# Attention score columns in a new order, one exp and three masks per step, and the rearrangement of Wo moved ahead in the DMA queue

## The chip, the cores and the metric

The kernel runs on one core of one Trainium2 chip. A time is the device time of one execution, in microseconds (us). The core has a matmul engine (PE; its weight loads are told apart as PEld), a vector engine (DVE), an engine for activation functions (ACT), a general one (POOL), and a queue engine (SP) that here does nothing but issue DMAs. The engines run on their own and wait for each other through semaphores.

## The reference

A block that adds three things: its input, sliding-window attention on the layer-normed input, and a gated linear unit (GLU) on the same normed input. There are 2048 positions, 640 features, 32 heads of 20, a window of 256 positions, and 1536 hidden features.

```python
xn = _layernorm(x)
# attention: H = 32, Dh = 20, W = 256
q, k, v = (xn @ wqkv) split into heads
scores = einsum("bhqd,bhkd->bhqk", q, k) * Dh ** -0.5
mask = (q_pos - k_pos >= 0) & (q_pos - k_pos < W)
p = softmax(where(mask, scores, -1e9))
attn = einsum("bhqk,bhkd->bhqd", p, v) reshaped to (B, S, D) @ wo
# GLU
h = sigmoid(xn @ w_gate) * (xn @ w_up)
return x + attn + h @ w_down
```

All data are bfloat16. B_x is not used.

## The kernel before, in words

**Chunks and fillers.** The 2048 positions are cut into four chunks of 512 (`c` = 0 to 3). Chunk 0 is normed, transposed and projected first (L601 to L633). Then one loop (L665 to L690) walks through the attention steps of all chunks and puts "filler" matmuls between them: the gate and up products (`g_gu`, L392), the q, k and v projections of the next chunk (`g_qk`, L360, and `g_v`, L375), and the down product with Wo's product added into the same PSUM tile (`g_out`, L448). The fillers stand in one list (L643 to L661), each with a cost in ns; a `credit` shared out evenly over the steps says how much of the list is taken after each step. A filler that only issues a DMA costs 0 and is taken when its turn in the list comes. So the order on every engine is fixed when the program is built, and each engine works its list off in order.

**Attention steps.** Four heads form a group `g`, and there are eight groups. A step takes scores between blocks of 128 keys and the queries they may see. Queries are counted in units of 64; a key block is used in halves of 64 keys (`hf` 0 and 1), which land in the lower and upper 64 partitions. One entry of `scores` is (group, half, key block relative to the chunk, first query unit, number of units, PSUM column unit), and becomes four matmuls, one per head, of 20 x 64 weights (L463). A step fills 8 column units for each of the four heads: the tile `ps`, four PSUM banks, of which there is one buffer. A chunk after the first has per pair of groups five steps: two "old" wide steps for each group, which also touch the previous chunk's keys, and one "full" step for both groups, which needs no mask. Chunk 0 has two wide steps per group. That makes 16 + 3 x 20 = 76 steps, 48 of them old wide ones.

**Exp and masks.** ACT takes `ps` through exp into the bfloat16 tile `pT` (L469), ten units wide; there are four buffers. In a wide step the first exp takes five units and the second three, which it writes one unit further on. POOL's `affine_select` (L473) then puts zeros where a key is later than the query or older than the window. `late` copies a masked unit to a unit of its own, since one unit holds scores of a first half of keys for one block and of a second half for another; `oldest` and `diag` mask in place. An old wide step has six masks (four of 64 columns per head, two of 128), a wide step of chunk 0 four.

**PV.** Two steps after a group's last one, `pv` (L489) multiplies V with the group's `pT` pieces: each entry of `pv` is (group, key block, first query unit, units, `pT` column unit) and becomes four matmuls with 128 x 32 weights, one per head, side by side in the array (L494). A column of constants beside V gives the softmax sums. DVE transposes the result, divides, and transposes back into `oc` (L502 to L520).

**DMAs.** All but three are issued by SP, in program order. q and k of a chunk are cast from PSUM into `st` (five buffers; q by DVE, L300, k by ACT, L302), stored to a scratch tensor in DRAM (`sq`, `sk`, L304), and read back with another spread over partitions (`spread`, L311). Wo's rows have to be put in the order in which `oc` holds the heads: `turn_wo` (L218) copies Wo inside DRAM to `wo_i`, four DMAs, and `load_wo` (L223) brings it into SBUF, four DMAs that wait for the first four. `load_wd` (L215) brings the down weights. In the list of fillers `turn_wo` stands after chunk 1's V projection and `load_wo` after the next two gate products, just ahead of `out0`, the first user of Wo.

Of the kernel before, what the change touches and what calls it, by code (L numbers as in the profile page):

```python
# [9 lines left out]
P = 128  # L10
# [7 lines left out]
CW = 512  # L18
NCH = S // CW
SBC = CW // P  # L20
HG = 4
# [6 lines left out]
SCALE = DH ** -0.5  # L28
# [14 lines left out]
U = 64  # L43
# [10 lines left out]

def wide_step(g, r, old):

    q = 2 * r  # L60
    scores = [(g, 0, r, q, 5, 0)]
    if old:
        scores += [(g, 1, r, q + 1, 5, 1), (g, 1, r - 2, q + 1, 1, 0), (g, 0, r + 2, q + 4, 2, 5),
                   (g, 1, r + 2, q + 5, 1, 6), (g, 1, r - 2, q, 1, 7), (g, 0, r - 2, q, 1, 7)]
        return dict(scores=scores, exps=[(0, 5, 0), (5, 3, 6)], late=[(0, 9), (6, 5)], diag=[0, 6],
                    oldest=[4, 8], pv=[(g, r, q, 6, 0), (g, r + 2, q + 4, 2, 6), (g, r - 2, q, 2, 8)],
                    units=8)

    scores += [(g, 1, r, q, 6, 0)]
    if r == 0:  # L70
        scores += [(g, 0, 2, 4, 3, 5), (g, 1, 2, 5, 2, 6)]
        last = [(g, 2, 4, 3, 6)]
    else:
        scores += [(g, 0, 3, 6, 2, 5), (g, 1, 3, 7, 1, 6), (g, 0, 2, 7, 1, 7), (g, 1, 2, 7, 1, 7)]
        last = [(g, 3, 6, 2, 6), (g, 2, 7, 1, 8)]
    return dict(scores=scores, exps=[(0, 5, 0), (5, 3, 6)], late=[(6, 5)], diag=[0, 6], oldest=[4],
                pv=[(g, r, q, 6, 0)] + last, units=8)


def full_step(gs):  # L80

    out = dict(scores=[], exps=[], late=[], diag=[], oldest=[], pv=[], units=8)
    for n, g in enumerate(gs):
        out["exps"].append((4 * n, 4, 4 * n))
        for r, q, col in ((-1, 0, 4 * n), (2, 6, 4 * n + 2)):
            out["scores"] += [(g, hf, r, q, 2, col) for hf in range(2)]
            out["pv"].append((g, r, q, 2, col))
    return out


def steps_of(c):
# [20 lines left out]
def kernel(  # L112
# [11 lines left out]
    nc = tc.nc  # L124
# [41 lines left out]
    wo = const.tile([P, DC, D], BF16, name="wo")  # L166
# [38 lines left out]
    wo_i = tc.dram_tile([HG, NG * DH, D], BF16, name="wo_i")  # L205
# [31 lines left out]
    for n in (7, 6):  # L237
        ps = ps_d.tile([P, CW], FP32, name="pwarm", tag="d")
# [50 lines left out]
    def proj_block(w, c, m):  # L289


        base = 0 if w == "q" else D
        ps = ps_d.tile([P, CW], FP32, name="pqk", tag="d")
        for d in range(DC):
            wt = wqkv[:, d, base:base + D].rearrange("p (k m) -> p m k", m=DC)
            nc.tensor.matmul(ps, lhsT=wt[:, m, :], rhs=xnT[c][:, d, :],  # L296
                             start=(d == 0), stop=(d == DC - 1))
        st = stp.tile([P, CW], BF16, name="st")
        if w == "q":
            nc.vector.tensor_copy(out=st, in_=ps)  # L300
        else:
            nc.scalar.copy(out=st, in_=ps)  # L302
        dst = scratch[w, c % 2].rearrange("(h j) s -> h j s", j=32)
        nc.sync.dma_start(out=dst[:, 4 * m:4 * m + 4, :], in_=st)  # L304
# [142 lines left out]
    def g_out(c):  # L447
        for s in range(SBC):  # L448
            ys = [ps_d.tile([P, CW], FP32, name=f"y{i}", tag="d") for i in range(2)]
            for y, cut in zip(ys, HALVES):  # L450
                yield from down(c, s, y, cut)
            outp(c, s, ys)
            yield 10 * 136


    def scores(c, step):
        pt = pp.tile([P, HG, PTW], BF16, name="pT")
        ps = ps_s.tile([P, HG, CW], FP32, name="ps")
        for g, hf, r, q, n, col in step["scores"]:
            kc, kb = divmod(c * SBC + r, SBC)  # L460
            key = kb * P + hf * U
            for i in range(HG):
                nc.tensor.matmul(  # L463
                    ps[hf * U:(hf + 1) * U, i, col * U:(col + n) * U],
                    lhsT=qk["k", kc][32 * i:32 * i + DH, g, key:key + U],
                    rhs=qk["q", c][32 * i:32 * i + DH, g, q * U:(q + n) * U],
                    start=True, stop=True)
        for col, n, to in step["exps"]:
            nc.scalar.activation(out=pt[:, :, to * U:(to + n) * U], in_=ps[:, :, col * U:(col + n) * U],  # L469
                                 func=EXP, scale=SCALE)  # L470

        def keep(out, in_, pattern, base, sign):
            nc.gpsimd.affine_select(out=out, in_=in_, pattern=[[0, HG], [sign, pattern]], compare_op=GE,  # L473
                                    fill=0.0, base=base, channel_multiplier=-sign)

        def cols(u, n):
            return pt[:, :, u * U:u * U + n]

        for a, b in step["late"]:
            keep(cols(b, U), cols(a, U), U, -1 - U, -1)  # L480
        for u in step["oldest"]:
            keep(cols(u, U), cols(u, U), U, -1, -1)
        for u in step["diag"]:
            keep(cols(u, P), cols(u, P), P, 0, 1)
        return pt

    def pv(c, g, parts):
# [175 lines left out]
    todo = [(c, k, step) for c in range(NCH) for k, step in enumerate(steps_of(c))]  # L663
# [9 lines left out]
    credit = 0  # L673
    fill.shut = {"out0", "out1", "out2"}
    for t, (c, k, step) in enumerate(todo):
        if k == 0 and c > 0:
            fill.until(f"qk{c}")
        if k == 2 and c > 0:
            fill.until(f"v{c}")
        for group in [x for x in ends if ends[x] == t - 2]:  # L680
            fill.flush()
            pv(*group, parts.pop(group))
            if group[1] == NG - 1:
                fill.shut.discard(f"out{group[0]}")
# [4 lines left out]
        credit += fill.left(label) * step["units"] / sum(x[2]["units"] for x in todo[t:last])  # L689
        credit = fill.pull(credit)  # L690
    fill.pull(10 ** 9)
    fill.flush()
# [61 lines left out]
```

## Time and profile before

| what | value |
|---|---|
| median of 5 runs | 317.62 us (317.17 to 319.85) |
| the profiled execution, its own time | 317.62 us |
| its span, first to last instruction | 315.7 us |
| granted clock of PE | 1.00 |
| busy: PE, ACT, POOL, DVE | 308.8, 198.0, 178.9, 154.3 us |
| L463 scores, matmuls | 2048 |
| L494 PV, matmuls | 928 |
| L469 exp, L473 masks, instructions | 152, 352 |

The profile page gives for each engine the busy time, its share of the span and its instructions; then the chain of work that ended last, and the costliest groups of instructions by source line. In a row of groups stand line, engine, operation, what it writes and reads, shapes and count, then the busy time in us, the mean of one in ns, and the idle time before them with what ended it. A row of waits says which instruction waited for which, the total in us, how often, and the longest. A row of the timeline has the start and the duration in us, engine, line, operation, tiles, shape and count; like instructions in succession are merged into one row, and an idle time ahead of it stands in brackets with what ended it. The duration of a matmul in these rows reaches beyond the start of the next one, because matmuls are pipelined; from one row's start to the next row's start is what the first one cost.

### The profile page before, as it was taken

Reading aid. Unit: us, or ns where it says so; the run is one execution under the profiler, and the core shown is the slowest. Engines: PE = TensorE matmul, PEld = TensorE weight load, DVE = VectorE, ACT = ScalarE, POOL = GpSimd, SP = SyncE. Lnnn points to the kernel's source line nnn. Section 1 sums busy time; section 2 is a strip of 40 time slices with the busy share of each in tenths; the row PEclk is TensorE's granted clock in tenths of the full one; section 3 lists DMA queues with packets and bytes.
Section 4 is the critical chain, followed back from the end, with each engine's and each line's share of the span. In section 5 each row is a group of like instructions: output and inputs, shape, how many; then the busy total and the mean of one; then the engine's idle time right before and its main releaser. Section 6 shows DMA issues by size and latency. Waiting matters only on the chain.

```text
span 315.7 us, 10314 instructions
## 1 busy us (share of the span) xinstructions
PE 308.8 (98%) x4410; PEld 175.2 (56%) x4410; DVE 154.3 (49%) x313; ACT 198.0 (63%) x255; POOL 178.9 (57%) x417
## 2 busy tenths in 40 slices
PE   7999999999979999999999999999999999999996
PEld 2654444456556655644466655544456664444674
DVE  3531486654854563347753542444552433563234
ACT  5724887788845458677744457776765658878200
POOL 3000487667758648565975647466365767676300
PEclk9999999999999999999999999999999999999999
DMA  7986958837735255410036025600000010000002
GB/s 254 374 292 190 334 191 131 302 92 208 249 102 65 50 172 153 157 65 2 0 43 88 23 87 142 227 3 2 3 3 23 25 42 3 2 2 2 0 2 83
DMA packets 34572, 33.05 MB, mean 105 GB/s; under 512 B 9920, under 2 KB 33984, under 8 KB 34496
## 3 DMA queue, kind: packets, MB, share of 16 engines
q1 hardware_dynamic: 34096, 32.14, 35.1%
q8 instruction: 34, 0.56, 0.8%
q10 hardware_dynamic: 432, 0.28, 0.3%
q14 instruction: 10, 0.08, 0.1%
HBM read 21.00 MB, written 10.26 MB: 99 GB/s over the span
## 4 chain that ended last, share of the span: by engine, by line
PE 89%; DMA 6%; ACT 2%; SPq 1%; issue 1%; DVE 0%; ACTq 0%
PE pu L403 16%; PE pg L396 16%; PE y L417 14%; PE pqk L296 13%; PE ps L463 8%; PE acc L494 7%; PE y L424 6%; PE pv L322 5%; DMA wo_i<-in_A_wo_dram 2%; PE d L417 2%; DMA sk<-st 1%; DMA wo<-wo_i 1%; DMA xc<-in_A_x_dram 1%; ACT pT L469 1%; SPq L220 1%
## 5 line engine op out<-in xcount | busy, mean ns | idle before, releaser
L473 POOL TENSOR_SCALAR_AFFINE_SELECT pT<-pT 128x256 bf16<-128x256 bf16 (+1 forms) x352 | 164.9, 502 | 115.0 <-ACT pT L469 114.8
L469 ACT ACTIVATE pT<-ps 128x1280 bf16<-128x1280 f32 (+2 forms) x152 | 147.4, 1022 | 64.9 <-PE ps L463 63.7
L407 DVE SCALAR_TENSOR_TENSOR h<-th,pu 128x512 bf16<-128x512 f32 x48 | 32.8, 684 | 56.6 <-PE pu L403 34.9
L396 PE MATMUL pg<-xnT,wg 128*128 128x512 bf16 x240 | 59.8, 380 | 0.0
L403 PE MATMUL pu<-xnT,wu 128*128 128x512 bf16 x240 | 59.8, 380 | 0.0
L417 PE MATMUL y<-wd,h 128*128 128x320 bf16 (+1 forms) x348 | 50.2, 297 | 0.0
L296 PE MATMUL pqk<-xnT,wqkv 128*128 128x512 bf16 x200 | 46.0, 381 | 0.0
L417 PEld LDWEIGHTS <-h 128*128 128x128 bf16 x396 | 36.7, 98 | 14.1 <-issue 0.2
L504 DVE STREAM_TRANSPOSE t<-acc 128x512 f32<-128x512 f32 x32 | 22.8, 712 | 33.5 <-PE acc L494 33.3
L399 ACT ACTIVATE th<-pg 128x512 f32<-128x512 f32 x48 | 28.8, 600 | 14.4 <-PE pg L396 7.7
L403 PEld LDWEIGHTS <-wu 128*128 128x128 bf16 x240 | 22.0, 98 | 25.4 <-issue 0.6
L396 PEld LDWEIGHTS <-wg 128*128 128x128 bf16 x240 | 22.0, 98 | 24.8 <-issue 0.4
L463 PEld LDWEIGHTS <-kT 20*64 20x64 bf16 x2048 | 22.1, 104 | 19.6 <-issue 16.2
L463 PE MATMUL ps<-qT,kT 20*64 20x64 bf16 (+3 forms) x2048 | 32.8, 232 | 0.0
L296 PEld LDWEIGHTS <-wqkv 128*128 128x128 bf16 x200 | 22.5, 119 | 17.9 <-issue 0.6
L428 DVE SCALAR_TENSOR_TENSOR xn<-y,xc 128x320 bf16<-128x320 f32 (+1 forms) x29 | 13.9, 483 | 31.2 <-PE y L424 31.1
L494 PE MATMUL acc<-pT,v 128*32 128x128 bf16 (+2 forms) x928 | 25.7, 250 | 0.0
L494 PEld LDWEIGHTS <-v 128*32 128x32 bf16 x928 | 16.9, 97 | 15.3 <-issue 11.0
L322 PE MATMUL pv<-wqkv,xnT 128*128 128x320 bf16 x160 | 23.8, 300 | 0.0
L424 PE MATMUL y<-wo,oc 128*128 128x320 bf16 (+1 forms) x145 | 21.6, 296 | 1.7 <-DMA wo<-wo_i 1.7
L516 DVE TENSOR_TENSOR on<-t,rec 128x320 bf16<-128x320 f32 (+4 forms) x48 | 20.9, 435 | 1.1
L424 PEld LDWEIGHTS <-oc 128*128 128x128 bf16 x165 | 15.5, 98 | 7.8 <-issue 2.0
(49 smaller groups left out, 148.8 us busy)
## 6 DMA issues: line engine op xcount, KB each, us to landing
qT<-sq SPq DMA_DIRECT2D x3, 1024.0 KB, 5.9
sq<-st SPq DMA_DIRECT2D x20, 128.0 KB, 3.5
sk<-st SPq DMA_DIRECT2D x20, 128.0 KB, 3.8
out_dram<-xn SPq DMA_DIRECT2D x15, 160.0 KB, 1.8
kT<-sk SPq DMA_DIRECT2D x3, 768.0 KB, 5.5
wg<-in_B_w_gate_dram SPq DMA_DIRECT2D x2, 960.0 KB, 7.1
wu<-in_B_w_up_dram SPq DMA_DIRECT2D x2, 960.0 KB, 12.3
xc<-in_A_x_dram SPq DMA_DIRECT2D x3, 640.0 KB
```

What stands on the lines that cost most here:

```text
L296: nc.tensor.matmul(ps, lhsT=wt[:, m, :], rhs=xnT[c][:, d, :], start=(d == 0), stop=(d == DC - 1))
L322: nc.tensor.matmul(ps[:, 0:HALF], lhsT=xnT[c][:, d, s * P:(s + 1) * P], rhs=wqkv[:, d, 2 * D + hf * HALF:2 * D + (hf + 1) * HALF], start=( ...
L396: nc.tensor.matmul(pg, lhsT=part(wg, d, f), rhs=xnT[c][:, d, :], start=(d == 0), stop=(d == DC - 1))
L399: nc.scalar.activation(out=th, in_=pg, func=TANH, scale=0.5)
L403: nc.tensor.matmul(pu, lhsT=part(wu, d, f), rhs=xnT[c][:, d, :], start=(d == 0), stop=(d == DC - 1))
L407: nc.vector.scalar_tensor_tensor(out=h, in0=th, scalar=1.0, in1=pu, op0=ADD, op1=MULT)
L417: nc.tensor.matmul(y[:, 0:cut[1] - cut[0]], lhsT=ht[c, f][:, s * P:(s + 1) * P], rhs=wd[:, f, cut[0]:cut[1]], start=(f == 0), stop=False)
L424: nc.tensor.matmul(y[:, 0:cut[1] - cut[0]], lhsT=oc[c, m][:, s * P:(s + 1) * P], rhs=wo[:, m, cut[0]:cut[1]], start=False, stop=(m == DC - 1))
L463: nc.tensor.matmul(ps[hf * U:(hf + 1) * U, i, col * U:(col + n) * U], lhsT=qk["k", kc][32 * i:32 * i + DH, g, key:key + U], rhs=qk["q", c] ...
L469: nc.scalar.activation(out=pt[:, :, to * U:(to + n) * U], in_=ps[:, :, col * U:(col + n) * U], func=EXP, scale=SCALE)
L473: nc.gpsimd.affine_select(out=out, in_=in_, pattern=[[0, HG], [sign, pattern]], compare_op=GE, fill=0.0, base=base, channel_multiplier=-sign)
L494: nc.tensor.matmul(acc[32 * i:32 * i + 32, q * U:(q + n) * U], lhsT=v[:, h * VW:h * VW + 32], rhs=pt[:, i, col * U:(col + n) * U], start=( ...
```

## The change

In `wide_step` the PSUM columns of an old step are ordered anew. Entries that were two narrow ones are merged, so that there are six score entries, three of them for each half of keys; the masked units now lie in pairs that are five units apart (`SPAN`), so one `affine_select` with a third pattern dimension covers two places. The exp is one instruction over all 8 units and writes `pT` units 0 to 7; units 8 and 9 hold the masked copies. The PV list has more and narrower entries: five for an old step (5, 2, 1, 1 and 1 units) where there were three (6, 2, 2), and one more in each wide step of chunk 0. A full step keeps its scores and PV entries and also gets one exp. In the list of fillers `turn_wo` moves from behind chunk 1's V projection to right behind `load_wd`, and `load_wo` from behind the two gate products to ahead of them. The credit is shared evenly per step, which it was already since every step had 8 units.

```diff
 def wide_step(g, r, old):
     q = 2 * r
-    scores = [(g, 0, r, q, 5, 0)]
     if old:
-        scores += [(g, 1, r, q + 1, 5, 1), (g, 1, r - 2, q + 1, 1, 0), (g, 0, r + 2, q + 4, 2, 5),
-                   (g, 1, r + 2, q + 5, 1, 6), (g, 1, r - 2, q, 1, 7), (g, 0, r - 2, q, 1, 7)]
-        return dict(scores=scores, exps=[(0, 5, 0), (5, 3, 6)], late=[(0, 9), (6, 5)], diag=[0, 6],
-                    oldest=[4, 8], pv=[(g, r, q, 6, 0), (g, r + 2, q + 4, 2, 6), (g, r - 2, q, 2, 8)],
-                    units=8)
+        return dict(scores=[(g, 0, r, q, 5, 1), (g, 1, r, q + 1, 5, 2), (g, 0, r + 2, q + 4, 2, 6),
+                            (g, 1, r - 2, q, 2, 0), (g, 0, r - 2, q, 1, 0), (g, 1, r + 2, q + 5, 1, 7)],
+                    late=(1, 8, 2), diag=1, oldest=(0, 2),
+                    pv=[(g, r, q, 5, 1), (g, r + 2, q + 4, 2, 6), (g, r, q + 5, 1, 9),
+                        (g, r - 2, q, 1, 0), (g, r - 2, q + 1, 1, 8)])
...
-        last = [(g, 3, 6, 2, 6), (g, 2, 7, 1, 8)]
-    return dict(scores=scores, exps=[(0, 5, 0), (5, 3, 6)], late=[(6, 5)], diag=[0, 6], oldest=[4],
-                pv=[(g, r, q, 6, 0)] + last, units=8)
+        last = [(g, 3, 6, 2, 5), (g, 2, 7, 1, 7)]
+    return dict(scores=scores, late=(5, 9, 1), diag=0, oldest=(4, 1),
+                pv=[(g, r, q, 5, 0), (g, r, q + 5, 1, 9)] + last)
...
-        for col, n, to in step["exps"]:
-            nc.scalar.activation(out=pt[:, :, to * U:(to + n) * U], in_=ps[:, :, col * U:(col + n) * U],
-                                 func=EXP, scale=SCALE)
-
-        def keep(out, in_, pattern, base, sign):
-            nc.gpsimd.affine_select(out=out, in_=in_, pattern=[[0, HG], [sign, pattern]], compare_op=GE,
-                                    fill=0.0, base=base, channel_multiplier=-sign)
...
-        for a, b in step["late"]:
-            keep(cols(b, U), cols(a, U), U, -1 - U, -1)
-        for u in step["oldest"]:
-            keep(cols(u, U), cols(u, U), U, -1, -1)
-        for u in step["diag"]:
-            keep(cols(u, P), cols(u, P), P, 0, 1)
+        nc.scalar.activation(out=pt[:, :, 0:CW], in_=ps, func=EXP, scale=SCALE)
+
+        def keep(out, in_, n, width, base, sign):
+            nc.gpsimd.affine_select(out=out, in_=in_, pattern=[[0, HG], [0, n], [sign, width]],
+                                    compare_op=GE, fill=0.0, base=base, channel_multiplier=-sign)
+
+        def spans(u, n, units):
+            a, b = divmod(u, SPAN)
+            two = pt.rearrange("p h (a b) -> p h a b", a=2)
+            return two[:, :, a:a + n, b * U:(b + units) * U]
+
+        if "late" in step:
+            src, to, n = step["late"]
+            keep(pt[:, :, to * U:(to + n) * U].rearrange("p h (n u) -> p h n u", u=U),
+                 spans(src, n, 1), n, U, -1 - U, -1)
+            u, n = step["oldest"]
+            keep(spans(u, n, 1), spans(u, n, 1), n, U, -1, -1)
+            keep(spans(step["diag"], 2, 2), spans(step["diag"], 2, 2), 2, P, 0, 1)
...
     fill.add("wd", later(load_wd), 0)
+    fill.add("wo_i", later(turn_wo), 0)
     fill.add("qk1", g_qk(1), 50 * MM)
     fill.add("v1", g_v(1), 40 * 136)
-    fill.add("wo_i", later(turn_wo), 0)
+    fill.add("wo", later(load_wo), 0)
     fill.add("gu1a", mix(g_gu(1, 0, 2), norms2, 0, 2, False), 2 * GU)
-    fill.add("wo", later(load_wo), 0)
     fill.add("out0", mix(g_out(0), norms2, 0, 2), OUT)
```

More of the change, by code (lines that the diff above doesn't have):

```diff
@@ L44 @@
 PTW = 10 * U
+SPAN = 5
 def wide_step(g, r, old):
     q = 2 * r
-    scores = [(g, 0, r, q, 5, 0)]
     if old:
-        scores += [(g, 1, r, q + 1, 5, 1), (g, 1, r - 2, q + 1, 1, 0), (g, 0, r + 2, q + 4, 2, 5),
-                   (g, 1, r + 2, q + 5, 1, 6), (g, 1, r - 2, q, 1, 7), (g, 0, r - 2, q, 1, 7)]
-        return dict(scores=scores, exps=[(0, 5, 0), (5, 3, 6)], late=[(0, 9), (6, 5)], diag=[0, 6],
-                    oldest=[4, 8], pv=[(g, r, q, 6, 0), (g, r + 2, q + 4, 2, 6), (g, r - 2, q, 2, 8)],
-                    units=8)
-    scores += [(g, 1, r, q, 6, 0)]
+        return dict(scores=[(g, 0, r, q, 5, 1), (g, 1, r, q + 1, 5, 2), (g, 0, r + 2, q + 4, 2, 6),
[3 more added lines that the diff above has]
+                        (g, r - 2, q, 1, 0), (g, r - 2, q + 1, 1, 8)])
+    scores = [(g, 0, r, q, 5, 0), (g, 1, r, q, 6, 0)]
     if r == 0:
         scores += [(g, 0, 2, 4, 3, 5), (g, 1, 2, 5, 2, 6)]
-        last = [(g, 2, 4, 3, 6)]
+        last = [(g, 2, 4, 3, 5)]
     else:
         scores += [(g, 0, 3, 6, 2, 5), (g, 1, 3, 7, 1, 6), (g, 0, 2, 7, 1, 7), (g, 1, 2, 7, 1, 7)]
-        last = [(g, 3, 6, 2, 6), (g, 2, 7, 1, 8)]
-    return dict(scores=scores, exps=[(0, 5, 0), (5, 3, 6)], late=[(6, 5)], diag=[0, 6], oldest=[4],
-                pv=[(g, r, q, 6, 0)] + last, units=8)
+        last = [(g, 3, 6, 2, 5), (g, 2, 7, 1, 7)]
+    return dict(scores=scores, late=(5, 9, 1), diag=0, oldest=(4, 1),
+                pv=[(g, r, q, 5, 0), (g, r, q + 5, 1, 9)] + last)
 def full_step(gs):
[L82 to L88, printed above, removed]
+    pieces = [(g, r, q, 2, 4 * n + col) for n, g in enumerate(gs) for r, q, col in ((-1, 0, 0), (2, 6, 2))]
+    return dict(scores=[(g, hf, *rest) for g, *rest in pieces for hf in range(2)], pv=pieces)
 def steps_of(c):
@@ L467, in scores @@
                     start=True, stop=True)
-        for col, n, to in step["exps"]:
-            nc.scalar.activation(out=pt[:, :, to * U:(to + n) * U], in_=ps[:, :, col * U:(col + n) * U],
-                                 func=EXP, scale=SCALE)
-        def keep(out, in_, pattern, base, sign):
-            nc.gpsimd.affine_select(out=out, in_=in_, pattern=[[0, HG], [sign, pattern]], compare_op=GE,
-                                    fill=0.0, base=base, channel_multiplier=-sign)
-        def cols(u, n):
-            return pt[:, :, u * U:u * U + n]
-        for a, b in step["late"]:
-            keep(cols(b, U), cols(a, U), U, -1 - U, -1)
-        for u in step["oldest"]:
-            keep(cols(u, U), cols(u, U), U, -1, -1)
-        for u in step["diag"]:
-            keep(cols(u, P), cols(u, P), P, 0, 1)
+        nc.scalar.activation(out=pt[:, :, 0:CW], in_=ps, func=EXP, scale=SCALE)
[13 more added lines that the diff above has]
+            keep(spans(step["diag"], 2, 2), spans(step["diag"], 2, 2), 2, P, 0, 1)
         return pt
@@ L688 @@
         last, label = next(x for x in cuts if t < x[0])
-        credit += fill.left(label) * step["units"] / sum(x[2]["units"] for x in todo[t:last])
+        credit += fill.left(label) / (last - t)
         credit = fill.pull(credit)
```

## The prediction

> **What bounds the kernel now.** The page's first part says that one engine fills the span:
>
> ```profile
> PE 308.8 (98%) x4410; PEld 175.2 (56%) x4410; DVE 154.3 (49%) x313; ACT 198.0 (63%) x255; POOL 178.9 (57%) x417
> ```
>
> A busy matmul engine is not proof that it is the bound, so next I read its own waits. There are three in the whole span, two of them in the first 8 us. The third is the only one in the steady part:
>
> ```profile
> PE y L424 <- DMA wo<-wo_i: 1.7, 1, 1.7
> ```
>
> The timeline of PE around it shows that the first output product of Wo found its weights not there:
>
> ```profile
> 87.66 0.99 PE L417 MATMUL y<-wd,h 128*128 128x320 bf16 x6
> 90.35 1.52 PE L424 MATMUL y<-wo,oc 128*128 128x320 bf16 x10 [1.70 <-DMA wo<-wo_i]
> ```
>
> The page counts 1.70 from the modelled end of the last L417 matmul (88.65). Matmuls overlap: six in a row start 0.137 apart, so the next would have started at 87.66 + 6 x 0.137 = 88.48. The wait costs 1.87. The rest of PE's time is work, and a change gains there only if PE's own stream gets shorter. ACT, POOL and DVE have idle time that no PE wait answers to.
>
> **The Wo rearrangement.** Now SP's queue, before and after the point where the change moves the four L220 issues:
>
> ```profile
> 52.32 0.49 SPq L216 DMA_DIRECT2D wd<-in_B_w_down_dram  x1
> 58.91 6.94 SPq L304 DMA_DIRECT2D sq<-st  x5
> ```
>
> ```profile
> 77.71 2.89 SPq L220 DMA_DIRECT2D wo_i<-in_A_wo_dram  x4
> 84.09 3.23 SPq L225 DMA_DIRECT2D wo<-wo_i  x4
> ```
>
> Gain: L220 moves from 77.71 to right behind wd (52.8), so wo no longer waits for wo_i. wo (L225) also moves ahead of the first gate products, directly behind the kT loads that SP issues until 77.7. Those fill the DMA engines until about 82 (share 1.07 at 80 to 81, 0.98 at 81 to 82, 0.50 after). wo then took 4 to 5 us from 85 on; from 82 it is there by 87, before PE needs it at 88.5 plus whatever is lost ahead. So the 1.87 go.
>
> Cost on SP: four issues take 2.89 and start at 52.8; SP is free at 55.7, and the first q store of chunk 1 is not ready until 58.9. Nothing on SP is late.
>
> Cost in the DMA queue: by one-microsecond windows its share is 1.0 to 1.1 from 54 to 61 and 0.64 in 61 to 62: x and wd drain until about 61.4. Today the first q stores follow at once. After the change the four wo_i pieces stand between. In the old place their landings released L225 at 84.1, 85.0, 86.0 and 87.0, one microsecond each. [...] An 8-row copy then uses 8 engines, and a store over 16 engines waits on those 8 behind all four pieces. If instead the pieces left the stores alone (the other 8 engines are free), the cost would be nothing. [...] Who waits for it? Its st buffer is one of five, and ACT's first k cast of this chunk takes the same buffer:
>
> ```profile
> 65.16 0.59 ACT L302 CAST st<-pqk 128x512 bf16<-128x512 f32 x1 [0.25 <-PE pqk L296]
> 66.30 1.94 ACT L469 ACTIVATE pT<-ps 128x1280 bf16<-128x1280 f32 x2 [0.55 <-PE ps L463]
> ```
>
> ```profile
> 68.31 0.42 PE L463 MATMUL ps<-qT,kT 20*64 20x320 bf16 x16
> ```
>
> [...] Bounds: 0 if the store lands by 65.8, and each microsecond later costs one; with the DMA engines lagging as they did at 82.8 to 86.6 (a landing at 67.0) it is 1.2. I take 0.5. Behind it ACT has slack again: the next score steps came at 71.56 and 74.74, over 3 us apart, against 1.9 of exp and 1.2 of casts. q and k of chunk 1 reach SBUF no more than about 0.5 later, and wo_i no longer stands behind them.
>
> **Score and PV matmuls on PE.** Counted from the code: each old wide step (48 of 76) has 24 score matmuls instead of 28 and 20 PV matmuls instead of 12; in chunk 0 (16 steps) 4 more PV matmuls each. PE gets 256 more matmuls. What does a set of four cost? Two stretches, a PV group and its next scores:
>
> ```profile
> 132.39 0.84 PE L494 MATMUL acc<-pT,v 128*32 128x384 bf16 x32
> 133.16 0.43 PE L463 MATMUL ps<-qT,kT 20*64 20x320 bf16 x28
> 133.53 0.39 PE L396 MATMUL pg<-xnT,wg 128*128 128x512 bf16 x1
> ```
>
> ```profile
> 59.17 0.68 PE L494 MATMUL acc<-pT,v 128*32 128x384 bf16 x20
> 59.77 0.43 PE L463 MATMUL ps<-qT,kT 20*64 20x320 bf16 x24
> 60.13 0.41 PE L296 MATMUL pqk<-xnT,wqkv 128*128 128x512 bf16 x1
> ```
>
> From start to start, PV with 32 matmuls (8 sets, 24 units of 64 columns) takes 0.77, with 20 (5 sets, 18 units) 0.60. The 6 more units are 384 columns; five matmuls of 512 columns take 1.08 from start to start, 0.42 ns a column, so 0.16 of it is columns and three more sets cost about 0.01, some 3 ns each. The change keeps the units and adds 4 sets per group in 24 groups and 2 in 8: 112 x 3 ns = +0.3. Scores take 0.37 with 28 matmuls and 0.36 with 24 (0.36 also with 16 or 32): the columns and the switch of tile shape set it. 48 steps x 0.008 = -0.4. Together -0.1.
>
> [...] No row shows PV sets of 64 columns in succession, of which there will be 168 instead of 8; score sets of 64 columns stand in succession inside the 0.36. [...]
>
> **Exp and masks.**
>
> ```profile
> L473 POOL TENSOR_SCALAR_AFFINE_SELECT pT<-pT 128x256 bf16<-128x256 bf16 x224 | 89.3, 424 | 115.0 <-ACT pT L469 114.8
> L469 ACT ACTIVATE pT<-ps 128x1280 bf16<-128x1280 f32 x64 | 79.2, 1238 | 55.9 <-PE ps L463 54.8 <-POOL pT L473 0.8
> L473 POOL TENSOR_SCALAR_AFFINE_SELECT pT<-pT 128x512 bf16<-128x512 bf16 x128 | 78.8, 640 | 0.0
> ...
> L469 ACT ACTIVATE pT<-ps 128x768 bf16<-128x768 f32 x64 | 51.7, 807 | 0.0
> ```
>
> Exp: 512 more elements cost 1238 - 807 = 431 ns, so 2048 take 1238 + 768 x 0.842 = 1.885, against 1.94 for today's pair. It starts no later: today's first exp begins 0.25 after the step's last score matmul too. So every exp ends 0.05 earlier. That matters where steps follow at 2.62 and the exp ends at 2.60 (133.16 + 2.60 = 135.77, next scores 135.79), but as PE does not wait there today, it gains nothing; were the exp 0.1 longer, some 25 such steps would wait. Masks: 256 elements 424, 512 elements 640, so 1024 about 1072. An old step goes from 4 x 424 + 2 x 640 = 2.98 to 640 + 640 + 1072 = 2.35, chunk 0 from 2.13 to 1.92. They now start when the whole exp is done, and end where they ended, about 5 us after the scores; PV comes two steps later (5.85 at the least). Cover: two step periods; hidden. Unknown is the third dimension of the pattern: nothing if it follows the elements; if it doubled them, 4 x 4.7 = 18.8 per five steps against 18.3 of PE would make POOL the bound, some +6.
>
> **Sum.** The profiled execution took 317.62 with a span of 315.7, and 317.62 is also the median of the runs. -1.87 (Wo) + 0.5 (st wait) - 0.1 (sets) = -1.5: 316.1.
>
> **Rivals.** (1) The st wait takes the place of the Wo wait: the pieces hold all stores back, the landing is at 67 or later, the stall 1.2 to 2: 316.9 to 317.7. For it: the DMA queue is full until 61.4 and the exp has 0.05 to spare; against it: half of the engines are free. (2) Slower: narrow PV sets do not run at 29 ns but at a floor. With 56 ns, what a 128-column set takes, 168 x 27 = 4.5: 320.6. It decides from 9 ns per set on (1.5/168). [...] (3) POOL's masks pay for the third dimension: about 322. (4) The Wo wait stays, since wo still queues behind kT, or oc comes late (DVE's transpose ends at 87.2, 1.2 before the need): 317.5.
>
> **How the numbers follow.** Main case 0.68 (315.3 to 316.9, just above and below the line of 0.5%, 316.0, about what a measurement of this kernel can tell); rival 1 0.12; rival 2 0.10; rival 3 0.04; rival 4 0.06. Faster by over 0.5%: 0.43, all from the main case. Slower by over 0.5% (above 319.2): most of 2 and 3, 0.12. Same: 0.45. The range 315.3 to 318.2 takes in main, 1 and 4 and leaves out 2 and 3.
>
> **What would show it.** No wait of L424 on wo; wo landed by 87. A wait of ACT's L302 on sq at about 65, and a gap of PE before the scores near 68.8. PV groups of 48 matmuls at 0.78 from start to start: over 0.9 makes rival 2 right. One exp per step at 1.88; masks of 640 and 1070. The prediction is wrong if PE waits in steps of 2.6 us period for the exp, or at PV for POOL.

## The result and the profile after

| | before | after |
|---|---|---|
| median | 317.68 us (80 runs, 316.84 to 321.46) | 316.39 us (43 runs, 315.54 to 319.28) |
| profiled execution, its own time | 317.62 us | 315.51 us |
| its span | 315.7 us | 313.8 us |
| granted clock of PE | 1.00 | 1.00 |

The ratio after to before is 0.9951, with a 95% interval of 0.9937 to 0.9965: 0.35 to 0.63% faster, with its middle 0.49%. A ratio here weighs all executions but those over 1.5% above the fastest of their kernel (two, of one experiment below), so it can differ from the quotient of the two medians, which is 0.9959: the kernel before has the longer tail, up to 321.46 us. The forecast was 316.1, with a range of 315.3 to 318.2. The time is in the range, 0.3 above the forecast; by its ratio it lies on the line of 0.5% that the forecast drew, by its median a little short of it. The profiled execution is among the fastest of its kernel, 0.9 under its median; the experiments tell most of why.

From the page of the changed kernel, the busy times and the exp:

```profile
PE 309.4 (99%) x4666; PEld 176.6 (56%) x4666; DVE 157.2 (50%) x313; ACT 193.3 (62%) x179; POOL 159.6 (51%) x257
...
L464 ACT ACTIVATE pT<-ps 128x2048 bf16<-128x2048 f32 x76 | 142.7, 1878 | 62.9 <-PE ps L459 58.5
```

PE has 256 more instructions and only 0.6 us more busy time. ACT has 76 exps, of 1878 ns each, instead of 152. POOL has 160 masks fewer and is busy 19 us less.

The groups of POOL, with different shapes kept apart:

```profile
L467 POOL TENSOR_SCALAR_AFFINE_SELECT pT<-pT 128x1024 bf16<-128x1024 bf16 x64 | 70.7, 1105 | 0.0
L467 POOL TENSOR_SCALAR_AFFINE_SELECT pT<-pT 128x512 bf16<-128x512 bf16 x96 | 63.0, 680 | 88.2 <-ACT pT L464 88.1
```

A mask over two places costs what its elements cost and little more: 680 where 512 elements took 640 in one place, 1105 where 1072 was worked out. (The 32 masks of 256 elements, in chunk 0, took 473 instead of 424.)

The waits of PE in the changed kernel have a single row, in the first 8 us:

```profile
PE pwarm L236 <- DVE st L165: 1.3, 1, 1.3
```

The row for L424 on wo (now L420) is gone, and no other stands in its place. The timeline of PE shows three places. The first is the scores that the prediction saw stalled, the second the first product of Wo, the third a PV group with its scores:

```profile
66.07 2.35 PE L292 MATMUL pqk<-xnT,wqkv 128*128 128x512 bf16 x10
68.54 0.42 PE L459 MATMUL ps<-qT,kT 20*64 20x320 bf16 x16
...
87.89 0.99 PE L413 MATMUL y<-wd,h 128*128 128x320 bf16 x6
88.72 1.52 PE L420 MATMUL y<-wo,oc 128*128 128x320 bf16 x10
...
130.73 0.85 PE L491 MATMUL acc<-pT,v 128*32 128x320 bf16 x48
131.52 0.43 PE L459 MATMUL ps<-qT,kT 20*64 20x320 bf16 x24
```

Wo's first product now follows the six down matmuls after 0.83, as matmuls in succession do: nothing is lost at the place that lost 1.87. But it was close. In the trace the last piece of wo landed at 88.46, 0.26 ahead of this product, and not by 87 as the prediction had it: fifteen DMA engines had delivered by 87.64, one was behind. At 68.54 there is no bracket, but ten matmuls of L292 do not take 2.47 from start to start. In the kernel before they took 2.28 there (66.03 to 68.31); so these scores started 0.19 late. This stall shows in the distance of the starts and not in the list of waits.

SP's queue after the change:

```profile
52.35 0.66 SPq L212 DMA_DIRECT2D wd<-in_B_w_down_dram  x1
53.06 3.75 SPq L216 DMA_DIRECT2D wo_i<-in_A_wo_dram  x4
58.95 6.50 SPq L300 DMA_DIRECT2D sq<-st  x5
...
78.50 0.88 SPq L307 DMA_DIRECT2D kT<-sk  x2
79.43 2.71 SPq L221 DMA_DIRECT2D wo<-wo_i  x4
```

The four pieces of Wo are issued ahead of the q stores, SP is free at 56.8, and the first store still leaves at 58.95. So SP itself loses nothing, and what the move costs has to be looked for behind SP, in the DMA engines. ACT shows it:

```profile
66.13 0.59 ACT L298 CAST st<-pqk 128x512 bf16<-128x512 f32 x1 [1.23 <-DMA sq<-st]
66.61 1.88 ACT L464 ACTIVATE pT<-ps 128x2048 bf16<-128x2048 f32 x1
```

The first k cast of chunk 1, at 65.16 before, waits for the first q store to give back its buffer. The exp behind it starts at 66.61 instead of 66.30, and its end at 68.49 is what the scores at 68.54 waited for. The trace has the landings of that store, one for each of 16 DMA engines: eight came by 63.3, the other eight from 65.35 to 66.03.

### The profile page after: what moved, and what is told of

It reads as the page before. It is cut to its first block, busy times and chain, and to the rows that moved or that the text cites. A ratio compares the mean times of both kernels' runs of the same rounds, so it can differ in the third digit from the quotient of the medians.

```text
span 313.8 us, 10571 instructions
## 1 busy us (share of the span) xinstructions
PE 309.4 (99%) x4666; PEld 176.6 (56%) x4666; DVE 157.2 (50%) x313; ACT 193.3 (62%) x179; POOL 159.6 (51%) x257
## 4 chain that ended last, share of the span: by engine, by line
PE 96%; ACT 1%; DMA 1%; DVE 1%; issue 0%
PE pg L392 17%; PE pu L399 17%; PE y L413 15%; PE pqk L292 14%; PE ps L459 9%; PE acc L491 8%; PE pv L318 7%; PE y L420 6%; PE d L413 2%; DMA xc<-in_A_x_dram 1%; PE d L420 1%; ACT pT L464 1%; PE pt L272 0%; PE acc L413 0%; ACT xn L588 0%; ACT xn L583 0%
## 5 line engine op out<-in xcount | busy, mean ns | idle before, releaser
L467 POOL TENSOR_SCALAR_AFFINE_SELECT pT<-pT 128x512 bf16<-128x512 bf16 (+2 forms) x192 | 145.3, 787 | 132.5 <-ACT pT L464 132.3
L464 ACT ACTIVATE pT<-ps 128x2048 bf16<-128x2048 f32 x76 | 142.7, 1878 | 62.9 <-PE ps L459 58.5
L292 PE MATMUL pqk<-xnT,wqkv 128*128 128x512 bf16 x200 | 46.0, 381 | 0.0
L292 PEld LDWEIGHTS <-wqkv 128*128 128x128 bf16 x200 | 22.5, 119 | 18.0 <-issue 0.6
L459 PE MATMUL ps<-qT,kT 20*64 20x128 bf16 (+4 forms) x1856 | 32.5, 239 | 0.1
L459 PEld LDWEIGHTS <-kT 20*64 20x64 bf16 x1856 | 20.7, 103 | 19.2 <-issue 15.8
L424 DVE SCALAR_TENSOR_TENSOR xn<-y,xc 128x320 bf16<-128x320 f32 (+1 forms) x29 | 13.9, 484 | 29.4 <-PE y L420 29.4
L491 PEld LDWEIGHTS <-v 128*32 128x32 bf16 x1376 | 19.5, 97 | 13.6 <-issue 11.0
L491 PE MATMUL acc<-pT,v 128*32 128x64 bf16 (+3 forms) x1376 | 26.0, 223 | 0.0
L513 DVE TENSOR_TENSOR on<-t,rec 128x320 bf16<-128x320 f32 (+4 forms) x48 | 22.2, 463 | 1.1
L420 PE MATMUL y<-wo,oc 128*128 128x320 bf16 (+1 forms) x145 | 21.6, 297 | 0.0
L296 DVE CAST st<-pqk 128x512 bf16<-128x512 f32 x20 | 13.7, 691 | 12.2 <-PE pqk L292 11.4
```

The costliest lines, as they stand in the source:

```text
L420: nc.tensor.matmul(y[:, 0:cut[1] - cut[0]], lhsT=oc[c, m][:, s * P:(s + 1) * P], rhs=wo[:, m, cut[0]:cut[1]], start=False, stop=(m == DC - 1))
L459: nc.tensor.matmul(ps[hf * U:(hf + 1) * U, i, col * U:(col + n) * U], lhsT=qk["k", kc][32 * i:32 * i + DH, g, key:key + U], rhs=qk["q", c] ...
L464: nc.scalar.activation(out=pt[:, :, 0:CW], in_=ps, func=EXP, scale=SCALE)
L491: nc.tensor.matmul(acc[32 * i:32 * i + 32, q * U:(q + n) * U], lhsT=v[:, h * VW:h * VW + 32], rhs=pt[:, i, col * U:(col + n) * U], start=( ...
```

## The experiments

Theory A is the prediction's: the gain is the Wo wait, a wait for an st buffer gives part of it back, and the new columns, exps and masks are worth about nothing. The rivals differ in what they charge to the columns, the masks and the st wait.

**The two halves of the change, apart.** The first kernel is the kernel before with the new place of Wo alone:

```diff
     fill.add("wd", later(load_wd), 0)
+    fill.add("wo_i", later(turn_wo), 0)
     fill.add("qk1", g_qk(1), 50 * MM)
     fill.add("v1", g_v(1), 40 * 136)
-    fill.add("wo_i", later(turn_wo), 0)
-    fill.add("gu1a", mix(g_gu(1, 0, 2), norms2, 0, 2, False), 2 * GU)
     fill.add("wo", later(load_wo), 0)
+    fill.add("gu1a", mix(g_gu(1, 0, 2), norms2, 0, 2, False), 2 * GU)
```

> The kernel before with nothing but the new places of the two Wo loads in the list of fillers. Theory A (the prediction's sum: all of the gain is the Wo wait, 1.87, less a stall behind the first q store): the wait of PE on wo is gone, ACT's first k cast of chunk 1 waits about 1.2 on sq, PE stalls there by 0.25 (the changed kernel's 0.19 and 0.06 for the longer pair of exps), profile about 316.0, ratio 0.995. Theory B (the new columns and the single exp give the gain): no change, 317.6, ratio 1.000.

Measured: 316.28 us against 317.37 of the kernel before on the same chip, ratio 0.9956 (0.9937 to 0.9976). That is all of what the whole change gives. In its profile, which at 317.23 is 0.95 above the median, nothing waits for wo, and the st wait is larger than in the profile of the whole change. From its waits of PE, and from its timeline of ACT:

```profile
PE ps L463 <- ACT pT L469: 1.3, 1, 1.3
```

```profile
67.27 0.59 ACT L302 CAST st<-pqk 128x512 bf16<-128x512 f32 x1 [2.31 <-DMA sq<-st]
```

Two rows of PE, 66.08 for the ten matmuls of L296 and 69.75 for the scores behind them, give the stall from start to start: 3.67 instead of 2.28, 1.39 lost. The first q store landed at 67.17 here, and at 66.03 in the profile of the whole change. Its sixteen landings show one DMA engine 0.9 behind the others. A packet of instructions, 1.07 us long, stood in one of the DMA engines at 60.78; the trace doesn't say in which, so that it was the late one is likely by the size and not shown. The size of the stall, at any rate, isn't fixed by the program.

The second kernel has the new columns, exps and masks, with Wo in its old place:

```diff
     fill.add("wd", later(load_wd), 0)
-    fill.add("wo_i", later(turn_wo), 0)
     fill.add("qk1", g_qk(1), 50 * MM)
     fill.add("v1", g_v(1), 40 * 136)
-    fill.add("wo", later(load_wo), 0)
+    fill.add("wo_i", later(turn_wo), 0)
     fill.add("gu1a", mix(g_gu(1, 0, 2), norms2, 0, 2, False), 2 * GU)
+    fill.add("wo", later(load_wo), 0)
```

> The changed kernel with the two Wo loads put back where they stood. Theory A: the wait on wo is back, 1.7 to 1.9; score groups 8 ns shorter and PV groups 10 ns longer cancel; 317.5, ratio 1.000. Theory B: 315.5 to 316.4, ratio 0.995.

Measured: 319.62 us, ratio 1.0051 (1.0029 to 1.0074; 319.62 and 317.37, the medians, would give 1.0071): slower than before, which theory A did not say. At first sight that speaks for the rival that makes the narrow sets dear. The timeline of PE says otherwise:

```profile
87.73 0.99 PE L413 MATMUL y<-wd,h 128*128 128x320 bf16 x6
90.96 2.33 PE L420 MATMUL y<-wo,oc 128*128 128x320 bf16 x10 [2.24 <-DMA wo<-wo_i]
93.08 1.81 PE L413 MATMUL y<-wd,h 128*128 128x320 bf16 x6
94.82 0.45 PE L459 MATMUL ps<-qT,kT 20*64 20x320 bf16 x24
```

Wo came later, so its product started 2.40 late instead of 1.87. After that ten matmuls took 2.12 from start to start (1.36 in the changed kernel) and the next six 1.74 (0.91 in a kernel where nothing waits there): 1.59 more for the same work. The windows of 2 us tell why; in each line stand the stretch and its length, the busy times of PE, PEld, DVE, ACT and POOL with their counts, then the granted clock, the DMA share and GB/s:

```profile
90.00:92.00 2.00, 1.04 (x6) 0.70 (x7) 0.01 (x1) 0.00 (x0) 1.13 (x3) 0.88 0.05 9
92.00:94.00 2.00, 2.00 (x9) 1.18 (x8) 1.16 (x3) 0.00 (x0) 0.00 (x0) 0.50 0.00 0
94.00:96.00 2.00, 2.00 (x34) 1.09 (x33) 0.53 (x2) 0.55 (x1) 0.00 (x0) 0.77 0.45 128
```

The granted clock fell to half behind the gap and came back at about 95. In the kernel before the same windows stand at 1.00, behind a gap of 1.70. So Wo's old place costs 1.87 in the one profile and 2.40 + 1.59 = 3.99 in the other. The difference, 2.1, is more than the 1.9 between the two spans (317.6 and 315.7): the columns themselves did not lose time. Wo came later in part because the kT loads ahead of it in SP's queue were issued at 77.92 instead of 76.77. They wait for the last two k stores, and one DMA engine landed these at 77.48 and 77.79, the others by 76.3. Here a packet of instructions can be placed: it stood from 75.36 to 76.32, and the last packets of the late engine start one after the other from 76.31 on, with none of any engine in the half microsecond before. (In the kernel before such a packet came at 75.83, and no engine was late.) Of these 1.15 us not all arrives: the last piece of wo was issued 0.36 later (87.38 against 87.02) and landed 0.60 later (90.82 against 90.22).

How often it happens, the mean clocks of the executions tell, as one stretch of half clock like this one, 3.4 us by the windows above, takes about 0.5% off the mean (0.5 x 3.4 / 317.6). 17 of the 22 executions of this kernel have a mean clock of 0.995 or less, all at 318.86 us or above, and the other five, at 0.999 or 1.0, took 317.05 to 318.72. Of the 59 executions of the kernel before beside them, 7 have 0.995 or 0.994, all at 319.3 or above; of the 43 of the changed kernel none is below 0.999. So the columns made an accident more frequent that the kernel before has in one execution of eight, and only while Wo stands in its old place. That the stretch lies behind the Wo wait in the others too, and that packets of instructions decide it, is not shown: only one was profiled.

**Wo earlier still.** The changed kernel with the rearrangement at the end of the first weight loads, where its DMAs stand before all of chunk 1's stores:

```diff
+        turn_wo()
...
-    fill.add("wo_i", later(turn_wo), 0)
```

> The changed kernel with the rearrangement of Wo issued still earlier, at the end of the first loads, ahead of the transposes of chunk 1 (so not behind the down weights). Theory A: the four pieces are through by about 48, the first q store of chunk 1 lands at about 63 as in the kernel before, the k cast no longer waits for sq, and PE's stall of 0.19 at the scores near 68.5 goes: profile about 315.3. If the spread of the changed kernel's runs (315.5 to 317.2) comes from that store, the median comes down to about 315.6, ratio 0.9935. Rival: the spread and the median have another cause and stay at 316.4; or the pieces delay the transposes of chunk 1 and the q projection at 56.9 waits.

Measured: 315.75 us, ratio 0.9939 (0.9921 to 0.9957). The k cast starts at 65.96 behind the projection and not behind a store: the st stall is gone, as it should be if the four pieces in the queue cause it. But the profile has two other DMA waits of PE in their place, 0.9 for up weights that the early pieces now delay and 0.4 for wo.

The same with load_wo moved up as well, ahead of the next chunk's x:

```diff
+    fill.add("wo", later(load_wo), 0)
     fill.add("x2", later(load_x, 2), 0)
...
-    fill.add("wo", later(load_wo), 0)
```

> The early rearrangement (at the end of the first loads) and the load of Wo into SBUF moved as well, ahead of x of chunk 2 and the down weights. Theory A: Wo is in SBUF by about 57 whatever the later landings are, so no execution waits for it; the first q store lands at 63 plus the 2 to 3 of Wo's load, 65 to 66, so that the k cast waits at most some tenths; 315.3, ratio 0.993, with fewer executions above 316.5 than with the changed kernel. Rival: the slower executions come from something else than the two waits and stay.

Measured: 316.03 us, ratio 0.9955 (0.9932 to 0.9978). Nothing waits for wo or for the up weights, but the st wait is back: the k cast starts at 66.95 after 2.04 of waiting, and the scores behind it lose 0.99 from start to start. So an early rearrangement alone doesn't keep the stores from being late: with load_wo moved ahead of them as well, the cast waited for the first one again.

**The st wait, made larger and taken away.** The changed kernel with the rearrangement done twice, the second copy into a tensor that nobody reads:

```diff
+    wo_j = tc.dram_tile([HG, NG * DH, D], BF16, name="wo_j")
...
-        for i in range(HG):
-            nc.sync.dma_start(out=wo_i[i].rearrange("(g d) n -> g d n", d=DH),
+        for t in (wo_i, wo_j):
+            for i in range(HG):
+                nc.sync.dma_start(out=t[i].rearrange("(g d) n -> g d n", d=DH),
```

> The changed kernel with the rearrangement done twice in its new place, the second time into a scratch tensor that nobody reads. Theory A (each engine takes its ring in order, stores wait behind the pieces on half of the engines): the first q store lands about 4 later (70 instead of 66), ACT's k cast waits some 5, PE stalls about 4.2 instead of 0.19: 319.5. Rival (the stores pass on the other engines, or the cast waits for something else): 315.5.

Measured: 321.97 us in one execution, span 320.3. From the timeline of PE:

```profile
72.56 0.65 PE L461 MATMUL ps<-qT,kT 20*64 20x320 bf16 x16 [4.19 <-ACT pT L466]
73.15 4.46 PE L294 MATMUL pqk<-xnT,wqkv 128*128 128x512 bf16 x10
```

The scores start at 72.56 instead of 68.35, a stall of 4.21: four more pieces cost 4.0 more than in the changed kernel, one microsecond each. ACT's k cast waits 5.31 for the store. The edit also did something that was not meant: SP, which waited 4.0 us for wd's landing among the extra issues, sent the first q store off at 63.55 instead of 58.95. The sixteen landings tell the two causes apart. Eight came by 65.90, some 2.4 after the issue, as eight of the changed kernel's did by 63.3; the other eight came from 69.14 to 69.99, 4.0 later than there. So SP's delay alone would have left the store's end where it was, and the size says what the pieces do: they pass one after the other through half of the engines, which the store needs too. In the trace of the changed kernel each piece has eight landings, the last of them at 62.86, 63.81, 64.78 and 65.71, just ahead of the store's last at 66.03. The total missed the expectation by 2.5, again because of the clock: from 72 to 78 it was granted at 0.50, and the scores and the ten matmuls in the two rows took 0.59 + 4.39 from start to start, where they take 0.36 + 2.29: 2.33 more. 313.8 - 0.19 + 4.21 + 2.33 = 320.15, within 0.2 of the span.

Then the wait taken away by its buffer. A sixth st buffer is paid for with one xn buffer less (at this and two more places):

```diff
-    stp = pool("stp", 5)
+    stp = pool("stp", 6)
...
-        xn = lnp.tile([P, D], BF16, name="xn", bufs=5)
+        xn = lnp.tile([P, D], BF16, name="xn", bufs=4)
```

> The changed kernel with six st buffers instead of five (and four buffers for normed rows instead of five, to make room), so that the first k cast of chunk 1 takes a buffer whose store landed long ago and the second one takes the first q store's. Theory A (PE's stall near 68.5 comes from that one cast waiting for the first q store, behind the pieces of Wo): ACT no longer waits for sq there, the stall of 0.2 to 1.4 is gone whatever the store's landing; median about 0.2 to 0.7 under the changed kernel's, 315.7. Rival: the stall is still there, as ps is held up by something else.

Measured: 315.43 us, all six runs between 315.31 and 315.89; ratio 0.9928 (0.9905 to 0.9951). From its timeline of ACT:

```profile
65.11 0.59 ACT L298 CAST st<-pqk 128x512 bf16<-128x512 f32 x1 [0.31 <-PE pqk L292]
```

The cast is back where it was before the change, with the four pieces still ahead of the stores and the first q store landing no sooner, at 66.23. For comparison the changed kernel itself ran again beside it:

> The changed kernel as it is, on the same chip as the last two, to compare them. 316.4 by its earlier runs, the profile with a wait of ACT's cast on sq of 1.2 or more and a PE stall of 0.2 to 1.4 near 68.5.

Measured: 316.5 us (315.36 to 317.83), ratio 0.9951 (0.9926 to 0.9975), as the first time. In this profile the cast started at 66.50 and the scores lost 0.50, against 0.19 in the first one. So the same program has a stall of 0.2 in one execution and 0.5 in another. The sixth buffer takes 1.07 off the median, and over six executions the spread is gone: about 1.0 is what the st wait costs in the middle execution of the changed kernel, with the fastest executions nearly free of it.

**The columns.** The changed kernel with all PV sets but the first of a group cut into single units, 20 or 23 sets in an old group instead of 12:

```diff
+        flat = [flat[0]] + [(pt, r, q + j, 1, col + j) for pt, r, q, n, col in flat[1:] for j in range(n)]
```

> The changed kernel with each PV entry but a group's first cut into entries of one unit (64 columns): 248 more sets of four matmuls, the same columns. Theory A (a set costs its columns and about 2.5 ns, its weight loads hidden): +0.6 to +0.8. [...] Rival, a set of 64 columns takes as long as one of 128 (56 ns): about +10. Rival, PE's sequencer can't issue so many: 192 and 48 instructions instead of 144 in a PV and score stretch, some us more.

Measured: 322.2 us in one execution, span 320.5. From the timeline of PE:

```profile
134.84 0.93 PE L492 MATMUL acc<-pT,v 128*32 128x320 bf16 x80
135.70 0.43 PE L459 MATMUL ps<-qT,kT 20*64 20x320 bf16 x24
```

The edit adds 284 sets and not the 248 of the expectation: in every second old group the first entry, which stays whole, is the full step's with two units, so that these groups get 23 sets. From start to start PV took 785 ns in 12 sets in the changed kernel, 859 in 20 and 880 in 23 (medians of 24, 12 and 12 groups), and in chunk 0 660 instead of 612 for seven more. An added set costs 7 to 9 ns. That is more than the 3 ns of the prediction. All sets together are 2.4 of the 6.7 us over the span of the changed kernel. The rest is waits that can't be laid to the sets: 1.2 for kT, 1.2 at the st stall, 0.8 for a transpose in chunk 0's V projection, and 0.6 in chunk 3's for which the profile names no cause. The kernel before had only one execution beside it, at 320.03.

The exp of a step cut into four:

```diff
-        nc.scalar.activation(out=pt[:, :, 0:CW], in_=ps, func=EXP, scale=SCALE)
+        for j in range(0, CW, 2 * U):
+            nc.scalar.activation(out=pt[:, :, j:j + 2 * U], in_=ps[:, :, j:j + 2 * U], func=EXP, scale=SCALE)
```

> The changed kernel with the exp of a step in four instructions of 2 units each instead of one. The four take about 4 x 0.594 less 3 x 0.1 of overlap, 2.08 instead of 1.88. Theory A (ps has one buffer, and 19 steps follow at 2.62 with the exp ending 0.11 to 0.2 ahead of the next scores, of which 0.05 is the semaphore): these steps now wait about 0.1 each, +1.5 to +2. Rival (ACT has a third of its time idle, so a longer exp is hidden): no change.

Measured: 317.12 us in one execution, span 315.4, 1.6 above the changed kernel's profile, as theory A said. Four exps end 2.06 after the first one's start, 0.18 later than one. No row of waits names the exp, but the two kernels have the same matmuls, so their starts can be laid beside each other: 19 score groups start 0.04 to 0.15 later behind the piece before them than in the changed kernel, 1.7 in sum. So the slack behind the exp is as small as the prediction read it, about 0.1 in the steps that follow each other fastest, and it is used up by 0.18.

Each mask for one place, as before, with the new columns:

```diff
-            keep(spans(u, n, 1), spans(u, n, 1), n, U, -1, -1)
-            keep(spans(step["diag"], 2, 2), spans(step["diag"], 2, 2), 2, P, 0, 1)
+            for j in range(n):
+                keep(spans(u + SPAN * j, 1, 1), spans(u + SPAN * j, 1, 1), 1, U, -1, -1)
+            for j in range(2):
+                u = step["diag"] + SPAN * j
+                keep(spans(u, 1, 2), spans(u, 1, 2), 1, P, 0, 1)
```

(and the late masks in the same way)

> The changed kernel with each paired mask as two (six in an old wide step, four in one of chunk 0), all else as changed. Theory A (POOL is off the path): no change, 315.5, POOL's busy time up from 160 to about 180, masks end some 0.6 later in each step. Rival: PV waits for POOL where a group's PV comes two short periods after its last masks, and the time rises by some tenths.

Measured: 316.39 us in one execution, span 314.7. POOL is busy 180.3 instead of 159.6, and no PV matmul waits for it. The 0.9 over the changed kernel's profile are two DMA waits: from start to start the scores at the st stall lose 0.48 instead of 0.19, and the first Wo product 0.61. So 21 us of POOL's time are worth nothing here, as predicted. The second wait is the prediction's fourth rival in small: wo landed at 89.48 here, and in three of the experiments' profiles it was 0.36 to 0.61 late.

**What the columns are worth, and the best version.** The kernel before with the new place of Wo and six st buffers, with the old columns, exps and masks:

> The kernel before with the two Wo loads in their new places and six st buffers, so the changed kernel's loads with the old columns, six masks and two exps. Theory A (new columns and single exp do nothing for PE: score groups 8 ns shorter, PV groups 10 ns longer): the same as the changed kernel with six buffers, 315.4 to 315.6. Theory B (they are worth some tenths through the exp's 0.06 in steps of 2.62): 315.7 or more.

Measured: 315.88 us (315.6 to 317.55) against 317.23, ratio 0.9953 (0.9936 to 0.9969), span 313.7. And the changed kernel with everything that helped: the rearrangement at the end of the first loads, load_wo ahead of the next chunk's x, six st buffers:

> All of Wo early and six st buffers together. Theory A: neither the wait on Wo (0.2 left in the profile with six buffers alone) nor the one on the first q store is left; PE's only waits are those before 8 us; span 313.6, 315.3, with hardly any spread. Rival: 2 to 3 us more of loads ahead of x of chunk 2 and of the stores delay q and k of chunk 1, and the first score step of chunk 1 waits; 315.5 or more.

Measured: 315.22 us (315.01 to 315.81), ratio 0.9915 (0.9882 to 0.9948), span 313.5. After the first 8 us PE waits for no DMA and for no buffer. This is the lowest median of the case, 2.0 under the kernel before on its chip, though its interval overlaps that of the changed kernel with six buffers. Two things remain to be told apart.

The columns. Old and new columns with six buffers each have intervals that overlap (0.9936 to 0.9969 and 0.9905 to 0.9951), so the medians don't settle what the columns are worth. The profiles do. Of all kernels with old columns and their counterparts with new ones the starts of the 275 stretches of PE can be laid beside each other. Four pairs (before and changed, before and the columns alone, old columns with six buffers against each of the two last kernels with new columns and six) give, without the first 8 us, the DMA waits, the st stall and the half clock, 0.29 to 0.31 us less for the new columns: 0.36 less in the scores, 0.28 more in PV, and 0.22 less in four places where with the old columns a matmul starts 0.02 to 0.09 late, too little to stand in the list of waits.

The sixth buffer. With the new columns it took 1.07 off the median (316.5 to 315.43, one chip). With the old ones it took 0.4 off (316.28 to 315.88, two chips, on which the kernel before took 317.37 and 317.23). So the st wait of the middle execution is smaller with the old columns; why, no run here shows.

## Why the prediction was right

**The bound.** Right. PE's own waits told where time could be had, and there was one place. "The rest of PE's time is work" is short of the truth by 0.22, the four small waits.

**The Wo gain of 1.87.** Right in the profiled pair: all of it is gone, and of the 1.9 between the spans 1.87 is this. The kernel with the Wo move alone has the whole gain. But the cover was thinner than worked out, and here luck helped: wo was to be there by 87, 1.5 ahead of the need, and it landed at 88.46, 0.26 ahead, since one DMA engine lagged. In other executions a part of the gain is lost again. And 1.87 holds for an execution at full clock; in the one profile where wo came 0.6 later, half clock followed, and the old place cost 3.99.

**The st wait of 0.5.** Right in mechanism: SP loses nothing, the store lands behind four pieces of about one microsecond, the k cast waits, the exp behind it starts late, the scores stall. The landing in the profile was at 66.03 and the sixteen landings fall into eight by 63.3 and eight from 65.35 on. In the traces of both kernels a piece of wo_i has eight landings and a store sixteen, so the store waited behind the pieces on eight of its engines, and the kernel with the pieces doubled gives this a size: 4.0 more for four more pieces. The term that was mis-sized is the 0.5 itself. It was the author's estimate, and no run shows it as a fixed cost; what the runs showed in its place is a quantity that was 0.19, 0.48 and 0.50 in three profiles with these loads and new columns and 1.39 in one with the old columns, and about 1.0 in the median of the changed kernel. With 1.07 for it and 0.30 for the columns the sum is -1.87 + 1.07 - 0.30 = -1.10; on the chip where the 1.07 was taken the medians differ by 1.12 (317.62 and 316.50). So the forecast was good in part by luck: a stall taken 0.6 too small and columns taken 0.2 too small. It also makes the profiled execution, with 0.19, 0.9 faster than the median. Rival 1 (a stall of 1.2 to 2, a landing at 67 or later) is what the Wo move alone showed in its profile; it is not another mechanism but the upper end of this one, and the bound of 1.2 was slightly low.

**Scores and PV, -0.1.** Right: from start to start the scores of an old step went from 367 to 359 ns, PV of an old group from 775 to 785 for four more sets, 2.5 ns a set against the 3 taken; in sum -0.36 + 0.28. Rival 2 with its 56 ns floor does not hold here. But the rival was nearer than the prediction's "3 ns" lets one think: with 20 or 23 sets in a row, nearly all of them of 64 columns, an added set costs 9 ns, which is where the rival would have decided. The row the 3 ns came from had sets of 128 columns; the change's three narrow sets per old step stand among wider ones, where an added set cost the 2.5.

**Exp and masks.** Right: 1878 ns against 1885, 680 and 1105 against 640 and 1072, and no wait for either. The third pattern dimension of rival 3 goes with 3 to 12% more per mask (1105 against 1072, 680 against 640, 473 against 424), not with twice as much. The warning that 0.1 more of exp would be felt in some 25 steps was borne out at 0.18, in 19.

**Rival 4.** Wrong for the profiled execution, by 0.26; a few tenths in others (0.36 to 0.61 for wo in three of the experiments' profiles).

## What to carry to other kernels

When a DMA is moved ahead in a queue, price what it is moved in front of (four more pieces put the store's end back by 4.0 us here): find the store whose buffer an engine will ask for next, and who waits behind that engine. One more buffer at that place was worth nearly as much as the change (1.07 us of median against 1.12 on that chip), though less with the old columns. And a wait of PE had two prices in two of the profiles here, its length and a half-clock stretch that followed (1.59 more behind 2.2 us, 2.33 more behind 4.2 us); a kernel that an edit to something else made slower may only have met such a stretch more often.

## What the runs showed of the hardware that was not expected

A gap of PE of 2.2 us was followed by half clock until about 4 us after work resumed (1.59 lost); one of 4.2 us by half clock that began in the gap and lasted until 5.4 us after it (2.3 lost); and one of 1.7 us by none. The granted clocks of the windows give the lengths. In the first case they are 0.88, 0.50 and 0.77 over 2 us each, (0.12 + 0.50 + 0.23) x 2 / 0.5 = 3.4 us of half clock; in the second 0.78, 0.50, 0.50 and 0.51 from 70 to 78, 6.8 us. The 2.2 us were enough in a stretch where PE had run without a wait before them. How long a gap has to be, and what sets the two lengths, no run here shows.

Packets of instructions go through the same DMA engines as the data, 0.88 to 1.64 us each in the kernel before. That they are PE's is read from their number: one queue carries 34 of them in the kernel before, 36 with 256 more matmuls and 45 with 1136 more again. In the kernel with the columns alone one of them held up its DMA engine, which landed the last stores 1.5 us behind the others, and so moved a wait of PE. Not every lag of one engine is explained by this: with the Wo move alone the first piece of wo has one 2.3 us behind the others, and no such packet stands between 78.7 and 86.6.
